# A Mamba-2 scan and a maxout FFN in one kernel: other places for scores and y, later quarter sums, a reordered load queue

## The chip, the cores and the metric

The kernel runs on one core of a Trainium2 chip. The metric is the device time of one execution in microseconds (us). Its engines are TensorE (PE in the profile, its weight loads PEld), VectorE (DVE), ScalarE (ACT), GpSimd (POOL) and SyncE (SP), which here only issues transfers. Each works through its own queue in order. Times of the kernel before: 297.39, 297.60 and 302.26 us, median 297.6.

## The reference, cut to what matters

Two blocks follow one another. The first is a chunked state-space scan over (batch 4, heads 8, sequence 768, head width 32), with a state of 16:

```python
for c in range(nc):                                   # chunks of the sequence
    cum = np.cumsum(log_a[chunk])
    L = np.exp(cum_i - cum_j) * causal                # decays
    M = (C @ B.T) * L                                 # scores, weighted
    y[chunk] = M @ x + (C @ state) * np.exp(cum)
    state = np.exp(sum(log_a)) * state + sum_j(B_j x_j * decay_from_j)
```

Its output, reshaped to 3072 tokens of 256 values, goes through a maxout FFN with d_ff = 768:

```python
h = np.maximum(np.maximum(x @ w1, x @ w2), x @ w3)
out = h @ w_out
```

The reference uses chunks of 32. The kernel takes chunks of 128 tokens, so there are NC = 6 of them.

## The kernel before

While chunk c goes through the FFN, the scan of chunk n = c + 1 is worked in between. For c = 1 to 5 a chunk takes NW = 9 *steps* k, each for two of the six blocks of d_ff and one of the three weight matrices. Chunk 0 goes before this loop; the point where the loop begins is called the seam below. The products of a step are Strassen-like: seven products in place of eight. Four of them come early and three late, and VectorE forms sums between:

```python
def early(c, k):
    A, B = (sum_bank(kind, [P, 2, HB]) for kind in "AB")      # PSUM banks: one of A, two of B
    products(c, k, [(1, A, 0), (6, A, 1), (5, B, 0), (7, B, 1)], True)        # L628
    ...
    nc.scalar.copy(out=eu[:, 0], in_=A[:, 0])                                 # L653
    nc.vector.tensor_tensor(out=eu[:, 1], in0=A[:, 1], in1=eu[:, 0], op=ALU.add)  # L654
    nc.vector.tensor_tensor(out=v, in0=B[:, 1], in1=eu[:, 1], op=ALU.add)     # L655
    nc.vector.tensor_tensor(out=t[:, 2], in0=B[:, 0], in1=v, op=ALU.add)      # L656

def late(c, k):
    products(c, k, [(2, A, 0), (3, B, 0), (4, B, 1)], False)                  # L628
    if i == 0:
        nc.scalar.copy(out=m[:, 0], in_=A[:, 0])                              # L667
    else:
        nc.vector.tensor_tensor(out=to[:, 0], in0=m[:, 0], in1=A[:, 0], op=ALU.max)   # L669
    nc.vector.tensor_tensor(out=t[:, 0:2], in0=B, in1=eu..., op=ALU.add)      # L670
    if i > 0:
        return [lambda: nc.vector.tensor_tensor(                              # L673
            out=to[:, 1:4], in0=m[:, 1:4], in1=t, op=ALU.max)]
    return []
```

What VectorE owes to the scan (score weightings, L491; sums of yT, L553; the state's sum, L462) and the maximum L673 go into a list `later`, from which each step takes a given number at three places (`pop`):

```python
def scan_weight(c, b0, r, s):                                   # L491, four to a group of scores
    M = Ls[c][:, b0:b0 + 2, 2 * r:2 * r + 2]
    nc.vector.tensor_tensor(out=M, in0=s, in1=M, op=ALU.mult)

def scores(n, b):
    for r, s in scan_scores(n, b).items():                      # TensorE, L483
        later.append(lambda r=r, s=s: scan_weight(n, b, r, s))
```

The down product (h @ w_out) is also one of seven products, in two halves u = 0, 1. Products 1, 6, 5 and 7 come first, then VectorE's *quarter sums*, then products 2, 3 and 4 into the same PSUM bank, then the rest of the sums and the store. The pieces of chunk c - 1 are handed out over the steps of chunk c, at the places marked "D":

```python
def quarter_sums(o, t):
    nc.vector.tensor_tensor(out=t[:, 0], in0=o[:, 1], in1=t[:, 1], op=ALU.add)   # L745
    nc.vector.tensor_tensor(out=t[:, 2], in0=o[:, 3], in1=t[:, 0], op=ALU.add)   # L746
    nc.vector.tensor_tensor(out=t[:, 3], in0=o[:, 2], in1=t[:, 2], op=ALU.add)   # L747

def output_products(c, u, which, kind=ffn_bank):
    if set(which) & {1, 2, 3, 4}:
        flush()                                                 # works off `behind`
    ...
    token_products(c, u, o, which)                              # L738
    if 7 in which:
        nc.scalar.copy(out=t[:, 1], in_=o[:, 0])                # L773
        behind.append(lambda: quarter_sums(o, t))
    if 4 in which:
        behind.append(lambda: output_rest(c, u, o, ob, t))      # L757, L759 and the store L786

downs.extend((c, u, which) for u, which in (
    (0, (1,)), (0, (6,)), (0, (5, 7)), (0, (2, 3, 4)), (1, (1, 6)), (1, (5, 7)), (1, (2, 3, 4))))
```

The loop, with its tables of places:

```python
X2 = ["t", "s0", "D", "D", "s2", "D", "y", "D", "D"]            # c = 2 to 4
...
for c in range(1, NC):
    for k in range(NW):
        early(c, k)
        part(n, ds[k][0]); part(n + 1, ds[k][1])                # decays: ScalarE's exps, L391
        pop(ps_[k][0])
        ...                                                     # xs[k]: D, t, s0, s2, A or y
        pop(ps_[k][1])
        maximum = late(c, k)
        ...
        if n < NC and k == 0:
            loads(c + 2)
        ...
        pop(ps_[k][2])
        flush()
        later[:0] = maximum
        if ys[k] == "D":
            down_next()
            flush()
        if k in ks and n + ks[k][0] < NC:
            decay_masks(n + ks[k][0], ks[k][1])                 # GpSimd, L384
    ...
last_output()
```

In X2, "t" is the transposes of B and C, "s0" and "s2" are the two groups of scores, and "y" is the scan's output with the state's product. Chunk 1 has its own tables X1 and P1.

Loads go through SyncE's queue in the order of the program. A tile of x has two buffers, so chunk 3's x can be loaded only when chunk 1's has been read for the last time, just ahead of the seam. The tiles of the decays and of B and C have two buffers as well:

```python
def load(c, name):
    src, w = sources[name]
    t = blocks[c][name] = raw.tile([P, BH, w], FP32, tag="raw_" + name, ...)   # bufs=2
    nc.sync.dma_start(out=t, in_=src[:, :, c * P:(c + 1) * P, :]...)           # L125

# chunk 0's FFN, n == 3:
    load(2, "B"); fetch(); load(2, "C"); fetch()
    decay_load(2, (0,)); last_load(2); decay_load(2, (2,)); load(2, "x")       # L372, L380

def loads(c):                                                   # from step 0 of the loop
    decay_load(c); last_load(c); load(c, "B"); load(c, "C"); load(c, "x")
```

And the end of the program, for the second half (u = 1) of the last chunk:

```python
    token_products(c, 1, o, (2, 3))
    nc.vector.tensor_tensor(out=t[:, 1], in0=o[:, 2], in1=t[:, 0], op=ALU.add)   # L855
    token_products(c, 1, o, (4,))
    nc.vector.tensor_tensor(out=t[:, 2], in0=o[:, 3], in1=t[:, 0], op=ALU.add)   # L857
    nc.sync.dma_start(out=rows[:, 3], in_=ob[:, 1])                              # L858
    nc.scalar.copy(out=t[:, 0], in_=o[:, 0])                                     # L859
    nc.scalar.dma_start(out=rows[:, 2], in_=ob[:, 0])                            # L860
```

Of the kernel before, what the change touches and what calls it, by code (L numbers as in the profile page):

```python
# [9 lines left out]
FP32 = mybir.dt.float32  # L10
# [3 lines left out]
ALU = mybir.AluOpType  # L14
# [5 lines left out]
def kernel(  # L20
# [20 lines left out]
    nc = tc.nc  # L41

    NB, NH, S, D = x.shape
    N = B.shape[-1]
    P = 128
    NC = S // P
# [3 lines left out]
    BH = NB * NH  # L50
# [8 lines left out]
    NQ = NF // 2  # L59
    HB = BLK // 2  # L60
# [5 lines left out]
    raw = ctx.enter_context(tc.tile_pool(name="raw", bufs=2))  # L66
    att = ctx.enter_context(tc.tile_pool(name="att", bufs=2))
    ffn = ctx.enter_context(tc.tile_pool(name="ffn", bufs=2))
# [16 lines left out]
    def att_bank(shape, name):  # L85
        turn["att"] += 1
        if shared["att"] and turn["att"] % 5 == 0:
            return bank("sumA", 1, shape, name)
        return bank("att", 4, shape, name)
# [10 lines left out]
    for k in range(REP):  # L100
# [5 lines left out]
        out=a_sb,  # L106
        in_=a_rows.rearrange("r (c i) -> (r c) i", i=P).rearrange("(w r) i -> r w i", w=2))
# [4 lines left out]
            name=nc.get_next_instruction_name(),  # L112
# [6 lines left out]
    blocks = {c: {} for c in range(NC)}  # L119
    sources = {"B": (B, N), "C": (C, N), "x": (x, D)}  # L120

    def load(c, name):
        src, w = sources[name]
        t = blocks[c][name] = raw.tile([P, BH, w], FP32, tag="raw_" + name, name="raw_" + name)
        nc.sync.dma_start(  # L125
            out=t, in_=src[:, :, c * P:(c + 1) * P, :].rearrange("b h s n -> s (b h) n"))

# [241 lines left out]
    def decay_load(c, pairs=(0, 2)):  # L369
        L = decays(c) if 0 in pairs else Ls[c]  # L370
        for b in pairs:
            nc.sync.dma_start(  # L372
                out=L[:, b:b + 2].rearrange("j b h i -> j (b h) i"),
                in_=cums[b * NH:(b + 2) * NH, c, :].partition_broadcast(P))
# [56 lines left out]
    def scan_cd(c):  # L431

        st = blocks[c]
        E = st["E"]
        st["Cd"] = Cd = att.tile([HN, NB, P], FP32, tag="Cd", bufs=1, name="Cd")
        nc.vector.tensor_tensor(out=Cd, in0=st["trC"], in1=E, op=ALU.mult)
# [197 lines left out]
    def pop(n):  # L634
        while n and later:
            later.pop(0)()
            n -= 1
# [91 lines left out]
    behind = []  # L729

    def flush():
        while behind:
            behind.pop(0)()

    def token_products(c, u, o, which, fs=range(NQ)):
        for p in which:
            for f in fs:
                nc.tensor.matmul(  # L738
                    out=o[:, PLACES[p]], lhsT=token_sums[c][p][:, f, u], rhs=wo_of(p)[:, f],
                    start=(p == 1 and f == 0), stop=True, skip_group_check=True)  # L740

    def quarter_sums(o, t):


        nc.vector.tensor_tensor(out=t[:, 0], in0=o[:, 1], in1=t[:, 1], op=ALU.add)  # L745
        nc.vector.tensor_tensor(out=t[:, 2], in0=o[:, 3], in1=t[:, 0], op=ALU.add)  # L746
        nc.vector.tensor_tensor(out=t[:, 3], in0=o[:, 2], in1=t[:, 2], op=ALU.add)  # L747

    def new_quarters(tag="ob"):
        if tag == "m":  # L750
            ob = ffn.tile([P, 4, HB], FP32, tag="m", name="m")[:, 0:2]
        else:
            ob = ffn.tile([P, 2, DM], FP32, tag="ob", bufs=2, name="ob")
        return ob, ob.rearrange("p b (m n) -> p (b m) n", n=P)
# [9 lines left out]
# [3 lines that stand above are left out]
        if 1 in which:  # L767
            halves[c, u] = kind([P, 4, P], "o")
        o = halves[c, u]
        token_products(c, u, o, which)  # L770
        if 7 in which:
            halves["ob", u] = ob, t = new_quarters()
            nc.scalar.copy(out=t[:, 1], in_=o[:, 0])  # L773
            behind.append(lambda: quarter_sums(o, t))
        if 4 in which:
            ob, t = halves["ob", u]
            behind.append(lambda: output_rest(c, u, o, ob, t))
# [57 lines left out]
    def last_output():  # L835
        c = NC - 1
        rows = out.rearrange("(b s) m -> s b m", s=S)[c * P:(c + 1) * P]
        hidden_sums(c, nc.vector, (NQ - 1, NQ))
        for u in range(2):
            third(c, u, NQ - 2)  # L840
        for p in (1, 5, 7, 6):
            for u in range(2):
                token_products(c, u, halves[c, u], (p,), (NQ - 1,))
        os = [halves[c, u] for u in range(2)]
        output_products(c - 1, 1, (4,))
        obs = [new_quarters(tag) for tag in ("ob", "m")]
        for o, (ob, t) in zip(os, obs):
            nc.scalar.copy(out=t[:, 1], in_=o[:, 0])
            quarter_sums(o, t)
        flush()  # L850
        token_products(c, 0, os[0], (2, 3, 4))
        output_rest(c, 0, os[0], *obs[0])
        o, (ob, t) = os[1], obs[1]
        token_products(c, 1, o, (2, 3))
        nc.vector.tensor_tensor(out=t[:, 1], in0=o[:, 2], in1=t[:, 0], op=ALU.add)  # L855
        token_products(c, 1, o, (4,))
        nc.vector.tensor_tensor(out=t[:, 2], in0=o[:, 3], in1=t[:, 0], op=ALU.add)  # L857
        nc.sync.dma_start(out=rows[:, 3], in_=ob[:, 1])  # L858
        nc.scalar.copy(out=t[:, 0], in_=o[:, 0])  # L859
        nc.scalar.dma_start(out=rows[:, 2], in_=ob[:, 0])  # L860


    for b in range(2, NB):
# [75 lines left out]

    def loads(c):  # L940
        if c < NC:
            decay_load(c)
            last_load(c)
            load(c, "B")
            load(c, "C")
            load(c, "x")

    def transposed(n, both=True):
        scan_b(n, att_bank)
# [9 lines left out]
    for n in range(NF * 3):  # L959
        j, g = divmod(n, 2)  # L960
        q, i = divmod(j, 3)
        f = 2 * q + g
        if n == 0:
            pair = [ffn_bank([P, BLK], "up") for _ in range(2)]
            group(pair[0], 0, 0, (0,))
            first_own((2, 3))
            group(pair[1], 0, 1, (0,))
            for p, ff in zip(pair, range(2)):
                group(p, 0, ff, (1,))
        if j > 0:  # L970
            p = ffn_bank([P, BLK], "up")
            whole_group(p, i, f)
        else:
            p = pair[g]
        if i == 0 and g == 0:
            m = ffn.tile([P, 4, HB], FP32, tag="m", name="m")
        if n in (13, 14, 16, 17):
            pop(2)
        mg = m[:, 2 * g:2 * g + 2].rearrange("p r t -> p (r t)")
        if i == 0:  # L980
            nc.scalar.copy(out=mg, in_=p)
        else:
            nc.vector.tensor_tensor(
                out=mg if i == 1 else h_of(0)[:, f], in0=mg, in1=p, op=ALU.max)
        if g == 0 and n <= 16:
            sign()
            if n <= 14:
                decode()
        if n == 1:
            fj = from_last(R, a_sb, "fj")  # L990
        if n == 3:
            first_tokens()
            load(2, "B")
            fetch()
            load(2, "C")
            fetch()
            decay_load(2, (0,))
            last_load(2)
            decay_load(2, (2,))
            load(2, "x")  # L1000
            decay_masks(1, (0, 1))
        if n == 9:
            decay_masks(1, (2, 3))
        if n in (5, 7, 9, 11, 13, 14, 15, 16):
            part(1)
        if n == 11:
            transposed(1)
            scan_c(1)
        if n == 12:
            scan_e(1)  # L1010
            scan_cd(1)
            scores(1, 0)
        if n == 15:
            shared["att"] = False
            scores(1, 2)
            places()
            weight_sums(0)
        if n == 17:
            decode()
            weight_sums(1)  # L1020
# [13 lines left out]

    X1 = ["tc", "D", "DD", "s0", "DD", "s2", "A", "y", "DD"]
    Y1 = ["", "", "D", "", "", "D", "", "D", ""]
    P1 = [(1, 0, 0), (1, 0, 0), (1, 0, 1), (1, 1, 2), (1, 0, 0), (1, 1, 3), (1, 1, 0), (1, 0, 0),
          (9, 0, 0)]
    D1 = [(0, 0), (0, 0), (2, 0), (2, 0), (2, 0), (2, 0), (0, 2), (0, 1), (0, 2)]
    K1 = {0: (0, (0, 1)), 2: (0, (2, 3)), 4: (1, (0, 1)), 6: (1, (2, 3))}  # L1040
    X2 = ["t", "s0", "D", "D", "s2", "D", "y", "D", "D"]
    Y2 = ["D", "D", "", "", "", "", "", "", ""]
    P2 = [(1, 0, 1), (1, 1, 1), (1, 0, 2), (1, 0, 0), (1, 1, 1), (1, 0, 2), (1, 0, 2), (1, 0, 2),
          (1, 0, 0)]
    D2 = [(0, 0), (1, 0), (1, 0), (1, 0)] + 5 * [(0, 1)]
    K2 = {3: (1, (0, 1)), 5: (1, (2, 3))}
# [2 lines left out]
    for c in range(1, NC):  # L1049
# [4 lines left out]
        for k in range(NW):  # L1054
# [48 lines left out]
            if n < NC and k == 2 * int(c == 1):  # L1103
                scan_e(n)
                later.append(lambda: scan_cd(n))
            pop(ps_[k][2])
            flush()
            later[:0] = maximum
            if ys[k] == "D":
                down_next()  # L1110
# [37 lines left out]
```

## Time and profile before

| | |
|---|---|
| time, median of 3 | 297.6 us |
| span of the profiled execution | 300.6 us |
| TensorE busy | 282.3 us (94%) |
| VectorE busy | 212.9 us (71%) |
| ScalarE, GpSimd busy | 119.5 us, 112.8 us |
| first step of chunk 1, 2, 3, 4, 5 in the loop | 65.1, 110.4, 157.1, 203.6, 248.8 us |
| last product ends, last store issued | 297.1, 297.8 us |

The profile is of one execution and counts from its first instruction. L628 is line 628 of the kernel before; tiles go by the program's names without buffer numbers, so `o<-wo,h` is a product of w_out and h written to a tile o. In a wait, the instruction named on the left stood at the head of its engine's queue, and the one on the right released it. The ends of matmuls are modelled in the profile, so distances are best taken from start to start.

### The profile page before, as it was taken

How to read it: one execution, taken by the hardware profiler on the slowest of the kernel's cores; microseconds unless marked ns; L12 is line 12 of the kernel's file. 1: busy time of each engine (PE TensorE's matmuls, PEld its weight loads, DVE VectorE, ACT ScalarE, POOL GpSimd, SP SyncE). 2: the span in 40 equal slices, each digit the busy share in tenths (PEclk: the TensorE clock that was granted, in tenths of full speed). 3: DMA queues.
4: the chain of work that ended last, by engine and by line, in shares of the span. 5: the costliest groups of instructions: out<-in, count | busy, mean ns of one | idle time of the engine just before them, and what ended most of it. 6: DMA issues, size and time to landing. Idle time of an engine off the chain costs nothing.

```text
span 300.6 us, 5773 instructions
## 1 busy us (share of the span) xinstructions
PE 282.3 (94%) x2204; PEld 225.9 (75%) x2204; DVE 212.9 (71%) x427; ACT 119.5 (40%) x323; POOL 112.8 (38%) x132
## 2 busy tenths in 40 slices
PE   6789999989999999899999999999989999999994
PEld 4556445478887878688977878888878888988984
DVE  2763878957789467868577868676778676677681
ACT  2946487743756345424426242525220201011101
POOL 5252656477990917900005920003530303030300
PEclk9969999999999999999999999999999999999999
DMA  7979879969787039950007690001001001000103
GB/s 90 227 248 320 181 132 178 255 173 206 210 96 106 2 96 250 106 77 2 2 0 219 145 139 27 3 0 37 0 0 37 2 1 35 2 1 0 37 0 105
DMA packets 105035, 28.15 MB, mean 94 GB/s; under 512 B 75312, under 2 KB 101936, under 8 KB 105008
## 3 DMA queue, kind: packets, MB, share of 16 engines
q1 hardware_dynamic: 104560, 27.53, 45.7%
q8 instruction: 17, 0.28, 0.4%
q10 hardware_dynamic: 448, 0.26, 0.3%
q14 instruction: 10, 0.08, 0.1%
HBM read 24.54 MB, written 3.24 MB: 92 GB/s over the span
## 4 chain that ended last, share of the span: by engine, by line
PE 77%; DVE 12%; issue 3%; DMA 3%; SPq 2%; ACT 1%; POOL 0%; DVEq 0%; ACTq 0%; POOLq 0%
PE sumB L628 22%; PE sumA L628 17%; PE o L738 15%; PE up L578 8%; PE s L483 4%; PE y L519 3%; DMA raw_x<-in_x_dram 3%; PE o L814 3%; DVE L L491 2%; PE y L506 2%; PE up L570 2%; DVE m L673 2%; PE y L530 1%; DVE rb L670 1%; SPq L125 1%
## 5 line engine op out<-in xcount | busy, mean ns | idle before, releaser
L628 PE MATMUL sumA<-yT,w 128*128 128x256 f32 x180 | 55.5, 390 | 1.4 <-DVE h L669 1.4
L653 ACT COPY eu<-sumA 128x256 f32<-128x256 f32 x45 | 16.8, 373 | 87.6 <-PE sumA L628 80.0
L391 ACT ACTIVATE L<-L,ncums 128x128 f32<-128x128 f32 x160 | 50.2, 392 | 2.5 <-POOL L L384 2.5
L628 PE MATMUL sumB<-rb 128*128 128x256 f32 x180 | 46.2, 379 | 0.0
L628 PEld LDWEIGHTS sumB<-rb 128*128 128x128 f32 x180 | 34.2, 190 | 4.7
L628 PEld LDWEIGHTS sumA<-yT,w 128*128 128x128 f32 x180 | 29.8, 190 | 9.0 <-DVE h L669 2.6
L654 DVE TENSOR_TENSOR eu<-sumA,eu 128x256 f32<-128x256 f32 x45 | 18.9, 420 | 18.9 <-ACT eu L653 18.5
L491 DVE TENSOR_TENSOR L<-s,L 128x512 f32<-128x512 f32 x46 | 29.8, 680 | 1.1 <-PE s L483 0.7
L578 PE MATMUL up<-yT,w 128*128 128x512 f32 x64 | 29.1, 600 | 0.2 <-DVE w L188 0.2
L670 DVE TENSOR_TENSOR rb<-sumB,eu 128x512 f32<-128x512 f32 x30 | 20.7, 690 | 10.4 <-PE sumB L628 10.3
L628 PE MATMUL sumB<-yT,rb 128*128 128x256 f32 x90 | 27.5, 387 | 0.6 <-DVE m L656 0.6
L185 POOL TENSOR_TENSOR w_u<-w_u,w_r 128x512 uint32<-128x512 uint32 x12 | 15.3, 1274 | 31.9 <-DVE w_u L179 15.5
L628 PE MATMUL sumB<-rb,w 128*128 128x256 f32 x90 | 26.8, 379 | 0.0
L628 PE MATMUL sumA<-rb 128*128 128x256 f32 x90 | 26.8, 379 | 0.0
L384 POOL TENSOR_SCALAR_AFFINE_SELECT L<-L 128x1024 f32<-128x1024 f32 x20 | 24.1, 1235 | 0.0
L470 POOL TENSOR_TENSOR S<-S,old 128x256 f32<-128x256 f32 x4 | 2.9, 726 | 56.2 <-DVE S L462 56.1
L713 POOL TENSOR_TENSOR L<-h 128x256 f32<-128x256 f32 x5 | 3.6, 726 | 52.2 <-DVE h L673 40.1
L655 DVE TENSOR_TENSOR v<-sumB,eu 128x256 f32<-128x256 f32 x45 | 19.1, 425 | 5.0 <-DVE eu L654 0.5
L578 PEld LDWEIGHTS up<-yT,w 128*128 128x128 f32 x64 | 11.6, 190 | 14.7 <-issue 11.7
L738 PE MATMUL o<-wo,h 128*128 128x128 f32 x120 | 17.5, 279 | 4.9 <-DVE ob L747 4.9
L738 PEld LDWEIGHTS o<-wo,h 128*128 128x128 f32 x120 | 15.9, 191 | 7.9 <-issue 5.0
L670 DVE TENSOR_TENSOR m<-sumB,eu 128x512 f32<-128x512 f32 x15 | 10.3, 690 | 15.4 <-PE sumB L628 15.3
(141 smaller groups left out, 512.5 us busy)
## 6 DMA issues: line engine op xcount, KB each, us to landing
L<-cums SPq DMA_DIRECT2D x10, 1024.0 KB, 8.8
rb<-in_moe_w_dram SPq DMA_DIRECT2D x9, 512.0 KB, 7.6
raw_x<-in_x_dram SPq DMA_DIRECT2D x6, 512.0 KB, 7.8
out_dram<-ob SPq DMA_DIRECT2D x11, 256.0 KB, 2.2
raw_B<-in_B_dram SPq DMA_DIRECT2D x6, 256.0 KB, 4.5
raw_C<-in_C_dram SPq DMA_DIRECT2D x6, 256.0 KB, 6.5
rb<-in_moe_w_out_dram SPq DMA_DIRECT2D x3, 512.0 KB, 6.0
E<-cums SPq DMA_DIRECT2D x40, 32.0 KB, 4.4
```

The costliest lines, as they stand in the source:

```text
L185: nc.gpsimd.tensor_tensor(out=u, in0=u, in1=r, op=ALU.add)
L384: nc.gpsimd.affine_select(out=Ls[c][:, b], in_=Ls[c][:, b], pattern=[[0, NH], [1, P]], compare_op=ALU.is_ge, fill=MASKED, base=0, channel_ ...
L391: nc.scalar.activation(L[:, b, h], L[:, b, h], AF.Exp, bias=ncum[c][:, b * NH + h:b * NH + h + 1], scale=1.0)
L483: nc.tensor.matmul(out=s[:, i].rearrange("j g i -> j (g i)"), lhsT=st["BT"][rows, b], rhs=st["CT"][rows, b].rearrange("p g i -> p (g i)"), ...
L491: nc.vector.tensor_tensor(out=M, in0=s, in1=M, op=ALU.mult)
L578: nc.tensor.matmul(out=bank, lhsT=w_sb[i][:, k, f * P:(f + 1) * P], rhs=yT[0][:, k], start=(k == 0), stop=(k == KD - 1))
L628: nc.tensor.matmul(out=bank[:, half], lhsT=left(p, k), rhs=sides[c][p], start=(first and half == 0), stop=True, skip_group_check=True)
L653: nc.scalar.copy(out=eu[:, 0], in_=A[:, 0])
L654: nc.vector.tensor_tensor(out=eu[:, 1], in0=A[:, 1], in1=eu[:, 0], op=ALU.add)
L655: nc.vector.tensor_tensor(out=v, in0=B[:, 1], in1=eu[:, 1], op=ALU.add)
L670: nc.vector.tensor_tensor(out=t[:, 0:2], in0=B, in1=eu[:, 1:2].to_broadcast([P, 2, HB]), op=ALU.add)
L738: nc.tensor.matmul(out=o[:, PLACES[p]], lhsT=token_sums[c][p][:, f, u], rhs=wo_of(p)[:, f], start=(p == 1 and f == 0), stop=True, skip_gro ...
```

## The change

It has four parts. In chunks 2 to 4 the second group of scores moves from step 4 to step 3, and y from step 6 to step 5. Products 2, 3, 4 of the first half of the down product then fall to step 4 and products 1, 6 of the second half to step 6. The flush that runs the quarter sums now comes ahead of a step's last pop, and is left out in step 2 of these chunks, so that the sums of the first half run at the end of step 3. The pops are arranged anew, in chunk 1 too. At the very end, product 4 of the last half goes to a PSUM bank of its own, the first quarter sum to a place of its own, and one copy and one store move ahead of it. Of the loads, chunk 2's x and the second half of its decays move from chunk 0's FFN to step 0 of the loop, behind chunk 3's x.

```diff
+    def home(c, name):
+        w = sources[name][1]
+        blocks[c][name] = raw.tile([P, BH, w], FP32, tag="raw_" + name, name="raw_" + name)
...
-    def token_products(c, u, o, which, fs=range(NQ)):
+    def token_products(c, u, o, which, fs=range(NQ), first=1):
...
-                    start=(p == 1 and f == 0), stop=True, skip_group_check=True)
+                    start=(p == first and f == 0), stop=True, skip_group_check=True)
...
-        nc.vector.tensor_tensor(out=t[:, 0], in0=o[:, 1], in1=t[:, 1], op=ALU.add)
-        nc.vector.tensor_tensor(out=t[:, 2], in0=o[:, 3], in1=t[:, 0], op=ALU.add)
+        nc.vector.tensor_tensor(out=w, in0=o[:, 1], in1=t[:, 1], op=ALU.add)
+        nc.vector.tensor_tensor(out=t[:, 2], in0=o[:, 3], in1=w, op=ALU.add)
... in last_output, w is t[:, 4] for u = 1; elsewhere t[:, 0]
-        nc.vector.tensor_tensor(out=t[:, 1], in0=o[:, 2], in1=t[:, 0], op=ALU.add)
-        token_products(c, 1, o, (4,))
-        nc.vector.tensor_tensor(out=t[:, 2], in0=o[:, 3], in1=t[:, 0], op=ALU.add)
+        nc.scalar.copy(out=t[:, 0], in_=o[:, 0])
+        nc.vector.tensor_tensor(out=t[:, 1], in0=o[:, 2], in1=t[:, 4], op=ALU.add)
+        nc.scalar.dma_start(out=rows[:, 2], in_=ob[:, 0])
+        o = att_bank([P, 4, P], "o")
+        token_products(c, 1, o, (4,), first=4)
+        nc.vector.tensor_tensor(out=t[:, 2], in0=o[:, 3], in1=t[:, 2], op=ALU.add)
         nc.sync.dma_start(out=rows[:, 3], in_=ob[:, 1])
-        nc.scalar.copy(out=t[:, 0], in_=o[:, 0])
-        nc.scalar.dma_start(out=rows[:, 2], in_=ob[:, 0])
...
     def loads(c):
         if c < NC:
+            if c == 3:
+                load(c, "x")
+                decay_load(2, (2,))
+                load(2, "x")
             decay_load(c)
             last_load(c)
             load(c, "B")
             load(c, "C")
-            load(c, "x")
+            if c > 3:
+                load(c, "x")
... chunk 0's FFN, n == 3
-            decay_load(2, (2,))
-            load(2, "x")
+            home(2, "x")
...
-    P1 = [(1, 0, 0), (1, 0, 0), (1, 0, 1), (1, 1, 2), (1, 0, 0), (1, 1, 3), (1, 1, 0), (1, 0, 0),
-          (9, 0, 0)]
+    P1 = [(1, 0, 0), (1, 0, 0), (1, 0, 1), (1, 1, 2), (1, 0, 0), (1, 1, 2), (1, 1, 1), (1, 0, 2),
+          (1, 0, 2)]
...
-    X2 = ["t", "s0", "D", "D", "s2", "D", "y", "D", "D"]
+    X2 = ["t", "s0", "D", "s2", "D", "y", "D", "D", "D"]
...
-    P2 = [(1, 0, 1), (1, 1, 1), (1, 0, 2), (1, 0, 0), (1, 1, 1), (1, 0, 2), (1, 0, 2), (1, 0, 2),
-          (1, 0, 0)]
+    P2 = [(1, 0, 1), (1, 1, 3), (0, 0, 1), (1, 1, 2), (1, 0, 0), (1, 0, 0), (9, 0, 0), (1, 0, 0),
+          (1, 0, 0)]
...
+            if not (1 < c < NC - 1 and k == 2):
+                flush()
             pop(ps_[k][2])
-            flush()
```

More of the change, by code (lines that the diff above doesn't have):

```diff
@@ L120 @@
     sources = {"B": (B, N), "C": (C, N), "x": (x, D)}
+    def home(c, name):
+        w = sources[name][1]
+        blocks[c][name] = raw.tile([P, BH, w], FP32, tag="raw_" + name, name="raw_" + name)
     def load(c, name):
-        src, w = sources[name]
-        t = blocks[c][name] = raw.tile([P, BH, w], FP32, tag="raw_" + name, name="raw_" + name)
+        if name not in blocks[c]:
+            home(c, name)
+        src, t = sources[name][0], blocks[c][name]
         nc.sync.dma_start(
@@ L739, in token_products, with quarter_sums @@
                     out=o[:, PLACES[p]], lhsT=token_sums[c][p][:, f, u], rhs=wo_of(p)[:, f],
-                    start=(p == 1 and f == 0), stop=True, skip_group_check=True)
-    def quarter_sums(o, t):
-        nc.vector.tensor_tensor(out=t[:, 0], in0=o[:, 1], in1=t[:, 1], op=ALU.add)
-        nc.vector.tensor_tensor(out=t[:, 2], in0=o[:, 3], in1=t[:, 0], op=ALU.add)
+                    start=(p == first and f == 0), stop=True, skip_group_check=True)
+    def quarter_sums(o, t, w):
+        nc.vector.tensor_tensor(out=w, in0=o[:, 1], in1=t[:, 1], op=ALU.add)
+        nc.vector.tensor_tensor(out=t[:, 2], in0=o[:, 3], in1=w, op=ALU.add)
         nc.vector.tensor_tensor(out=t[:, 3], in0=o[:, 2], in1=t[:, 2], op=ALU.add)
@@ L750, in new_quarters @@
         if tag == "m":
-            ob = ffn.tile([P, 4, HB], FP32, tag="m", name="m")[:, 0:2]
+            ob = ffn.tile([P, 4, HB], FP32, tag="m", name="m")
         else:
@@ L773, in output_products @@
             nc.scalar.copy(out=t[:, 1], in_=o[:, 0])
-            behind.append(lambda: quarter_sums(o, t))
+            behind.append(lambda: quarter_sums(o, t, t[:, 0]))
         if 4 in which:
@@ L846, in last_output @@
         obs = [new_quarters(tag) for tag in ("ob", "m")]
-        for o, (ob, t) in zip(os, obs):
+        for o, (ob, t), place in zip(os, obs, (0, 4)):
             nc.scalar.copy(out=t[:, 1], in_=o[:, 0])
-            quarter_sums(o, t)
+            quarter_sums(o, t, t[:, place])
         flush()
```

## The prediction

> **What bounds the kernel now.** I read the page first. TensorE is busy 94% of the span and no other engine over 71%, so a change can win time only where TensorE stands still.
>
> ```profile
> span 300.6 us, 5773 instructions
> PE 282.3 (94%) x2204; PEld 225.9 (75%) x2204; DVE 212.9 (71%) x427; ACT 119.5 (40%) x323; POOL 112.8 (38%) x132
> ...
> PE   6789999989999999899999999999989999999994
> ...
> PEclk9969999999999999999999999999999999999999
> ```
>
> The PE row, one digit for each 7.5 us, shows idle time in the first slices, in the ninth (60 to 67.5 us), thinly through the chunk loop, and in the last slice. The clock row dips to 6 in the third slice; the profiled execution took 302.3 us against a median of 297.6, and the change touches nothing there, so I count down from 297.6.
>
> Second, the waits of TensorE (engine, line and tile that waited, what released it: us in total, times, longest):
>
> ```profile
> PE o L738 <- DVE ob L747: 4.9, 7, 1.2
> ...
> PE o L814 <- issue: 1.5, 1, 1.5
> PE sumA L628 <- DVE h L669: 1.4, 3, 0.7
> ...
> PE sumB L628 <- DVE m L656: 0.6, 3, 0.3
> PE o L738 <- DVE m L855: 0.4, 1, 0.4
> ```
>
> The largest is the output product behind the quarter sums (L745 to L747). Third, the timeline around one such wait, TensorE first, then VectorE (start, length, operation; the bracket is the idle time ahead of it):
>
> ```profile
> 125.92 1.03 PE L628 MATMUL sumB<-rb 128*128 128x256 f32 x4
> 127.69 0.91 PE L738 MATMUL o<-wo,h 128*128 128x128 f32 x6 [0.74 <-DVE ob L747]
> ```
>
> ```profile
> 122.96 1.61 DVE L673 TENSOR_TENSOR m<-m,rb 128x768 f32<-128x768 f32 x1
> 124.50 0.41 DVE L669 TENSOR_TENSOR h<-m,sumA 128x256 f32<-128x256 f32 x1
> 124.83 0.68 DVE L670 TENSOR_TENSOR rb<-sumB,eu 128x512 f32<-128x512 f32 x1
> 125.43 1.27 DVE L491 TENSOR_TENSOR L<-s,L 128x512 f32<-128x512 f32 x2
> 126.62 0.27 DVE L745 TENSOR_TENSOR ob<-o,ob 128x128 f32<-128x128 f32 x1
> 126.93 0.29 DVE L746 TENSOR_TENSOR ob<-o,ob 128x128 f32<-128x128 f32 x1
> 127.25 0.29 DVE L747 TENSOR_TENSOR ob<-o,ob 128x128 f32<-128x128 f32 x1
> ```
>
> VectorE has no idle time here: a maximum, two score weightings and then the quarter sums stand in one queue, and products 2, 3, 4 come one step after products 5, 7, so TensorE arrives first.
>
> **What the Trainium skill says.** "TensorE: Matmul & The Clock Gate", section "Step-by-step: what each phase is for", says that only weight loads are pulled ahead and matmuls stay in program order. The trace agrees: at 127.69 the later sums, which need nothing of L747, wait too. "PSUM — Partial Sum Buffer", section "PSUM bank collisions raise a hardware error", has accesses of two engines guarded by bank, not by address. The program does so: at 296.20 product 4 waits 0.39 us for L855, which reads another quarter of the bank. "SBUF — State Buffer", section "Who interferes with whom", says that a VectorE operation with two SBUF inputs contends with a GpSimd one that reads SBUF. That fits the maximum L673: 1.61 us at 122.96 while GpSimd masks, 0.95 elsewhere. "DMA: Bandwidth & Descriptors", section "Latency and other measured facts", has HBM latency grow under load; I use it only for a rival.
>
> **Part 1: places in chunks 2 to 4 (c = 2, 3, 4).** A wait costs more than its bracket. Undisturbed, the four products of sumB are followed 0.87 us after their start; at 127.69 it was 1.77, so 0.90 lost. The same subtraction at the other five gives 0.82 (153.25), 0.89 (174.23), 0.82 (199.79), 1.34 (220.56) and 0.48 (245.37): 5.25. After each, six products took 0.74 us start to start, against 0.67: another 0.4. Together **5.7 us**. For u = 0 products 2, 3, 4 move from step 3 to step 4, with the scores between. For u = 1 the distance stays, but the sums are flushed ahead of what step 7 pops (two operations of about 0.33 us, once one), and that pop is now 0. Both should go.
>
> The maximum L673 of step 1 leaves the front of step 2, so L669 comes earlier and the products of step 3 no longer wait for it (124.96 and 171.50): start to start 0.92 and 0.99 instead of 0.43, with 0.1 each for the slower pair after: **1.2 us**.
>
> What it adds: VectorE must do in step 3 what lay over steps 2 to 4. I count from step 3's first product, with times of this trace. An undisturbed step has 1.75 us of early products, 1.30 of late ones, VectorE's eu at about 1.55 and its third sum finished 1.41 later; a score group takes 1.08. On VectorE: L670 of step 2 to 0.8, the moved maximum to 1.7, eu/v/t to 3.1, step 2's maximum to 3.9, one weighting (0.6) to 4.5, L670 to 5.1, quarter sums (0.92) to 6.0, two weightings to 7.2. TensorE starts step 4 at 4.2 and wants products 2, 3, 4 at 5.95: a wait of 0 to 0.1. The next eu starts at 7.2, its third sum is done at 8.6, and the late products of step 4 can want it at 8.4: 0.2. If the maximum meets GpSimd's masks (0.65 longer, chunks 2 and 3 only), about 0.6 more. So 0.3 to 0.9 in each of two chunks, 0.3 in the third: **1.5 us given back**.
>
> y comes a step earlier, with its four sums and the state's in step 6: five at 0.33, so eu of step 7 begins about 0.5 late, its third sum at 7.85 on a clock from step 6, when the late products want it at 7.87. Quarter sums then finish at 10.35, wanted at 10.47. Tight, but no wait.
>
> **Part 2: chunk 1's pops.** One weighting and the state's sum move behind the sums of step 6, and the four sums of yT are split between the ends of steps 7 and 8. L628's waits at 96.85 (0.33) and 110.42 (0.73) are behind exactly these. By starts: 0.49 + 0.08, and 0.89 + 0.1: **1.6 us**. The third yT sum must be ready 1.3 us into the next chunk and ends at about 1.25; I take 0.1 off.
>
> **Part 3: the end.** Product 4 of the last half gets a bank of its own, so it starts at 295.65 (0.67 after 294.98) instead of 296.20. Its sum ends at about 296.9, and the copy that ran after it (L859, 0.27) and its store move ahead. Before, the last store is issued at 297.80; now the last is at 296.9. They land in 1.7 and 1.8 us. **0.9 us.**
>
> **Part 4: the transfers.** Same bytes, other order. Before, half of chunk 2's decays is issued at 64.28, its x at 64.70, and chunk 3's x at 87.22. Now chunk 3's x goes first and waits for chunk 1's last readers (TensorE at 62.1). The two others move about 1.8 us later, the time from 64.70 to the next issue at 66.51. The masks of that half start at 79.44, x is used at 95.24; with about 9 us to land both have room. Expected: 0.
>
> Sum: 5.7 + 1.2 + 1.6 + 0.9 - 1.5 - 0.1 = 7.8 us. 297.6 - 7.8 = 289.8; I round to **290.0**.
>
> **Rivals.** *VectorE's backlog takes the wait's place.* From step 2 to step 4 it has about 13 us of work in 13.5 us of TensorE. For it: L673 at 1.61, the margins of 0.1 us above. Against: VectorE is busy 34.5 of 46.6 us in a chunk, and early in steps 5 and 7 it has slack. It would leave 3 to 4 us of the gain: 293.5 to 294.5. *The transfers are the real gain.* TensorE stands still for 1.48 us at 63.2 with no releaser, while the DMA share was 1.17 in the 2 us before; if that is instruction fetch (the page lists instruction queues among the DMA's) behind data, moving data behind the seam could free it: 288.5. Against: before, both moved transfers were issued only at 64.28 and later, when the gap was nearly over. *They do harm*: chunk 2's masks come late; 2 us at most, 292. *The waits are hidden anyway*, by clock or VectorE: then 296. Against it is the timeline, where every later start shifts.
>
> **Range and chances.** 2% is 291.65 us, a gain of 5.95. The sum holds unless given-back time exceeds 3.4 us in place of 1.6. I take **287.2 to 294.0** for 8 in 10, and chances of 0.68 faster, 0.31 within 2% and 0.01 slower: nothing adds work, so only a chain of new waits could lose.
>
> **What would show it.** Right: the wait of o on ob falls from 4.9 us to under 1 and is left only in the last output; L669's three waits go; a chunk of the loop falls from 46.6 us (110.42 to 157.06) to about 44.5; the last store is issued about 1.3 us after product 4's start, with no copy behind it. Wrong: a new line of TensorE on L656, L669 or the quarter sums in steps 3 to 7 of 1 us per chunk (rival 1); the gap at the seam gone (rival 2); a wait of GpSimd's masks or of TensorE for a DMA between 65 and 95 us (rival 3). What would make it wrong above all is the count of VectorE's backlog, where I add up margins of 0.1 us by hand.

## The result and the profile after

The changed kernel takes 291.07 us (median of 5) against 297.62 (median of 5): ratio 0.9772, 95% interval 0.9753 to 0.9792, so 6.2 to 7.3 us less. Some executions of every kernel here took about 5 us longer, and where one of them was profiled, as for before and after, the TensorE clock was near 0.5 for part of the time from 15 to 28 us and 1.0 from there on, so the ratios leave them out and the traces are compared behind that.

The page after, head and TensorE's row of 40 slices:

```profile
span 294.2 us, 5768 instructions
PE 283.0 (96%) x2204; PEld 226.0 (77%) x2204; DVE 214.0 (73%) x427; ACT 119.6 (41%) x323; POOL 113.4 (39%) x132
...
PE   6679999999999999999999999999999999999995
```

The slices of the loop are full, and the dent in the ninth is gone. The waits of TensorE after (us in total, times, longest; the first, for x, ends at 15.5 us, ahead of everything that was changed); lines are five or so higher, so L743 is L738 and L661 is L656:

```profile
PE A L456 <- DMA raw_x<-in_x_dram: 1.9, 1, 1.9
...
PE o L743 <- DVE ob L752: 1.0, 3, 0.6
...
PE sumB L633 <- DVE m L661: 0.3, 2, 0.2
```

The wait on the quarter sums fell from 4.9 us to 1.0, of which 0.57 lies in the last output. The three waits on L669, the one at the seam and the one in the end are gone.

Where the time came from, between the first products of step 0 of one chunk and the next, in us. (For before, the true first products of chunks 3 and 4 are at 156.63 and 203.17; the marks 157.06 and 203.60 used ahead are their second pair.)

| chunk | before | after | less |
|---|---|---|---|
| 1 | 45.3 | 44.2 | 1.1 |
| 2 | 46.2 | 44.7 | 1.5 |
| 3 | 46.5 | 45.1 | 1.4 |
| 4 | 45.6 | 44.1 | 1.5 |
| first L745 of the last output to last store issued | 6.65 | 5.70 | 0.95 |

Together 6.5 us, which is the timed difference. (From there to the last output both take 42.4 us.) The seam can't be read from this pair: chunk 1 begins at 65.10 and 65.18, but the trace before has a gap of 1.48 us ahead of it, and the trace after lost about as much earlier, 0.7 us of it in a longer wait for x (1.9 us against 1.2). The run with the transfers alone, below, settles it.

How steps 3 and 4 of chunk 2 look now, TensorE first and then VectorE:

```profile
126.26 0.70 PE L633 MATMUL sumA<-yT,w 128*128 128x256 f32 x2
126.90 0.70 PE L633 MATMUL sumB<-yT,rb 128*128 128x256 f32 x2
...
128.73 1.03 PE L633 MATMUL sumB<-rb 128*128 128x256 f32 x4
129.98 0.94 PE L743 MATMUL o<-wo,h 128*128 128x128 f32 x6 [0.22 <-DVE ob L752]
```

```profile
124.17 1.35 DVE L678 TENSOR_TENSOR m<-m,rb 128x768 f32<-128x768 f32 x1
...
126.76 1.12 DVE L678 TENSOR_TENSOR h<-m,rb 128x768 f32<-128x768 f32 x1
127.80 0.68 DVE L496 TENSOR_TENSOR L<-s,L 128x512 f32<-128x512 f32 x1
128.40 0.68 DVE L675 TENSOR_TENSOR m<-sumB,eu 128x512 f32<-128x512 f32 x1
129.00 0.27 DVE L750 TENSOR_TENSOR ob<-o,ob 128x128 f32<-128x128 f32 x1
```

VectorE runs on without a break from one maximum to the next, and the quarter sums, though a step away from the products 5, 7 that they follow, are still not in time: from 128.73 to 129.98 is 1.25, against 0.87 undisturbed.

### The profile page after: what moved, and what is told of

Same layout as the page of the kernel before. It is cut to its first block, busy times and chain, and to the rows that moved or that the text cites. A ratio compares the mean times of both kernels' runs of the same rounds, so it can differ in the third digit from the quotient of the medians.

```text
span 294.2 us, 5768 instructions
## 1 busy us (share of the span) xinstructions
PE 283.0 (96%) x2204; PEld 226.0 (77%) x2204; DVE 214.0 (73%) x427; ACT 119.6 (41%) x323; POOL 113.4 (39%) x132
## 3 DMA queue, kind: packets, MB, share of 16 engines
q1 hardware_dynamic: 104560, 27.53, 46.5%
## 4 chain that ended last, share of the span: by engine, by line
PE 84%; DVE 7%; DMA 3%; SPq 2%; issue 1%; ACT 1%; POOL 0%; DVEq 0%; ACTq 0%; POOLq 0%
PE sumB L633 25%; PE sumA L633 18%; PE o L743 16%; PE up L583 8%; PE s L488 4%; PE o L819 4%; PE y L524 3%; DMA raw_x<-in_x_dram 3%; PE y L511 2%; PE up L575 2%; PE y L535 1%; SPq L130 1%; PE A L456 1%; DVE rb L675 1%; DVE m L678 1%
## 5 line engine op out<-in xcount | busy, mean ns | idle before, releaser
L633 PEld LDWEIGHTS sumB<-yT,rb 128*128 128x128 f32 x90 | 15.8, 189 | 6.0 <-DVE m L661 2.3
L743 PEld LDWEIGHTS o<-wo,h 128*128 128x128 f32 x120 | 15.9, 191 | 4.0 <-DVE ob L752 1.6
L633 PEld LDWEIGHTS sumA<-rb 128*128 128x128 f32 x90 | 17.1, 190 | 2.3
```

What stands on the lines that cost most here:

```text
L633: nc.tensor.matmul(out=bank[:, half], lhsT=left(p, k), rhs=sides[c][p], start=(first and half == 0), stop=True, skip_group_check=True)
L743: nc.tensor.matmul(out=o[:, PLACES[p]], lhsT=token_sums[c][p][:, f, u], rhs=wo_of(p)[:, f], start=(p == first and f == 0), stop=True, skip ...
```

## The experiments

**Each part alone.** Four kernels, each the one before with one part of the change. For each, what was expected, then the edit and what was measured. The us less are one minus the ratio, times 297.5.

The end alone:

> The kernel before with part 3 alone (product 4 of the last half in its own bank, the copy and one store ahead of it). My theory: 0.9 us less, all of it behind the last quarter sums (from the first L745 sum of the last output to the last store issued: 5.7 us instead of 6.65), nothing elsewhere. If the end were hidden behind the stores' landing, 0 to 0.3 us.

```diff
+        nc.scalar.copy(out=t[:, 0], in_=o[:, 0])
+        nc.vector.tensor_tensor(out=t[:, 1], in0=o[:, 2], in1=t[:, 4], op=ALU.add)
+        nc.scalar.dma_start(out=rows[:, 2], in_=ob[:, 0])
+        o = att_bank([P, 4, P], "o")
+        token_products(c, 1, o, (4,), first=4)
```

Ratio 0.9961 (0.9948 to 0.9974): 0.8 to 1.5 us less. The expectation of 0.9 stands, and from the first quarter sum of the last output to the last store issued it is 5.71 us (285.82 to 291.53).

The transfers alone:

> The kernel before with part 4 alone (chunk 3's x first, chunk 2's x and half of its decays behind it). My theory: 0, within 0.4 us, and if the 1.48 us gap of TensorE at the seam is missing in the profile it is not this that removed it. Rival (the transfers are the gain): 1.5 us less, and the gap gone here while it stays in the runs that keep the old load order. Rival (they do harm): 0.5 us or more slower, with a wait for masks or a DMA between 65 and 95 us.

```diff
+            if c == 3:
+                load(c, "x")
+                decay_load(2, (2,))
+                load(2, "x")
```

Ratio 0.9998 (0.9989 to 1.0008): nothing, within 0.3 us. The gap at the seam, in the profile before, then its place here:

```profile
64.67 0.59 PE L814 MATMUL o<-wo,h 128*128 128x256 f32 x2 [1.48 <-issue]
```

```profile
58.47 0.66 PE L415 MATMUL trB<-ident,raw_B 128*128 128x128 f32 x4
58.96 1.03 PE L819 MATMUL o<-wo,h 128*128 128x256 f32 x4
```

Here it is missing, but it is missing as well in the run with only the end changed, which has the old load order:

```profile
58.50 0.66 PE L410 MATMUL trB<-ident,raw_B 128*128 128x128 f32 x4
58.99 1.03 PE L814 MATMUL o<-wo,h 128*128 128x256 f32 x4
```

Of all profiles of this study with the old load order, the profile before alone has the gap. So the old order does not bring it about each time, and the timed runs show no cost of it. What made TensorE stop there in that execution is open.

The places of chunks 2 to 4 alone:

> The kernel before with part 1 alone (places and pops of chunks 2 to 4, the flush ahead of the last pop and left out in step 2). The changed kernel's profile shows chunks 2 to 4 in 44.7, 45.1 and 44.1 us instead of 46.6, 46.5 and 45.2, so 4.4 us less less what of it came from chunk 1's last wait; I expect 4.0 to 4.4 us less. If VectorE's backlog from elsewhere set these waits, under 3 us.

```diff
-    X2 = ["t", "s0", "D", "D", "s2", "D", "y", "D", "D"]
+    X2 = ["t", "s0", "D", "s2", "D", "y", "D", "D", "D"]
... and P2 and the flush, as in the change
```

Ratio 0.9862 (0.9842 to 0.9882): 3.5 to 4.7 us less, the middle 4.1. Chunks 2 and 3 take 44.8 and 45.2 us, as in the changed kernel.

Chunk 1's pops alone:

> The kernel before with part 2 alone (the pops of chunk 1). My theory: 1.3 to 1.6 us less, the waits of TensorE for L656 in step 6 and for L669 in step 8 of chunk 1 gone. If chunk 1 is bound by its load and decode work instead, 0 to 0.5 us.

```diff
-    P1 = [..., (1, 1, 3), (1, 1, 0), (1, 0, 0), (9, 0, 0)]
+    P1 = [..., (1, 1, 2), (1, 1, 1), (1, 0, 2), (1, 0, 2)]
```

Ratio 0.9972 (0.9944 to 0.9999): 0.0 to 1.7 us less. One of the nine executions behind it, 300.03 us, makes the interval wide; the other eight took 295.7 to 296.6 us, on average 1.3 less than the kernel before. The trace agrees: chunk 1 takes 44.2 us (65.21 to 109.39) against 45.3, so 1.1, and chunk 2 another 0.1. The wait for L669 in step 8 is gone; of the wait for L656 in step 6 a rest stays (below).

The four come to 1.2 + 0.1 + 4.1 + 0.8 = 6.2 us (6.7 with 1.3 for the pops), against 6.8 for the whole: nothing of weight arises from their working together.

**Is it the places, or the order of VectorE's queue?** The scores between products 5, 7 and products 2, 3, 4 give the quarter sums more time, but the same edit also takes the pop out of their way.

> The kernel before, every place and pop as it was, with one edit: the flush that runs the quarter sums stands ahead of a step's last pop, in every step. If the distance between products 5, 7 and products 2, 3, 4 is what took the wait away (part 1 as I told it), only the second halves gain: about 0.6 us in each of three chunks, 1.8 us. Rival: what stood between was the pop, two weightings of 0.6 us each, longer than the wait of 0.7 to 1.2 us; then the first halves gain as well and it is 3.5 to 4.1 us less, as much as the moved places gave (4.1), with the two waits on L669 in step 3 still there.

```diff
-            pop(ps_[k][2])
             flush()
+            pop(ps_[k][2])
```

Ratio 0.9849 (0.9827 to 0.9871): 4.5 us less, with every place and pop as before. The rival holds: no wait of o on ob is left in the loop, and the waits on L669 are still there (1.5 us). TensorE and VectorE in step 3 of chunk 2:

```profile
121.55 1.03 PE L628 MATMUL sumB<-rb 128*128 128x256 f32 x4
122.42 0.83 PE L738 MATMUL o<-wo,h 128*128 128x128 f32 x6
```

```profile
120.45 0.68 DVE L670 TENSOR_TENSOR rb<-sumB,eu 128x512 f32<-128x512 f32 x1
121.06 0.27 DVE L745 TENSOR_TENSOR ob<-o,ob 128x128 f32<-128x128 f32 x1
...
121.90 1.28 DVE L491 TENSOR_TENSOR L<-s,L 128x512 f32<-128x512 f32 x2
```

The two weightings now stand behind the quarter sums, and product 2 starts 0.87 us after sumB's products: no wait. In the profile before they stood ahead, 1.19 us of work (125.43 to 126.62), as much as the longest of the waits (1.19). Small losses stay: step 8 takes about 5.27 us in each of the three chunks, where 5.03 is undisturbed. No run moves the places and leaves the flush behind the pop, so what the distance alone would bring is not shown; shown is that the flush does it without the distance.

**Load or order?** The same question put more sharply: in most steps VectorE has idle time just ahead of L670, as in step 7 of chunk 2 before:

```profile
150.90 0.69 DVE L670 TENSOR_TENSOR rb<-sumB,eu 128x512 f32<-128x512 f32 x1 [0.44 <-PE sumB L628]
```

Not so in step 2, where the first half's sums are due: there the long maximum makes L669 late, and L670 follows at once (124.50, 124.83).

> The kernel before, places and pops as they were, with one edit: the quarter sums are flushed inside the step, between L669 and L670, where VectorE sat idle 0.44 us for the late products of sumB. If VectorE's order and not its load bounds these chunks, the waits of o on ob in the loop go to under 0.1 us each, 5 to 5.7 us less, more than the moved places gave (4.1). If its load bounds them, the later L670 is paid back in the next step's sums, and it is 4 us or under.

```diff
             nc.vector.tensor_tensor(out=to[:, 0], in0=m[:, 0], in1=A[:, 0], op=ALU.max)
+        flush()
         nc.vector.tensor_tensor(
             out=t[:, 0:2], in0=B, in1=eu[:, 1:2].to_broadcast([P, 2, HB]), op=ALU.add)
```

Ratio 0.9788 (0.9767 to 0.9809): 5.7 to 6.9 us less, at or above the 5 to 5.7 expected. This one line, with every place and pop as before, gives nearly what the whole change gave. In step 2 of chunk 2 the sums did not fill idle time: they went ahead of L670 and of two weightings, none of which TensorE then waited for.

```profile
125.16 0.28 DVE L746 TENSOR_TENSOR ob<-o,ob 128x128 f32<-128x128 f32 x1
...
126.01 0.68 DVE L671 TENSOR_TENSOR rb<-sumB,eu 128x512 f32<-128x512 f32 x1
126.61 1.28 DVE L491 TENSOR_TENSOR L<-s,L 128x512 f32<-128x512 f32 x2
```

```profile
126.26 1.03 PE L628 MATMUL sumB<-rb 128*128 128x256 f32 x4
127.12 0.83 PE L739 MATMUL o<-wo,h 128*128 128x128 f32 x6
```

The work is the same and only its order changed, so order it is, not load. Part of the surplus over the expectation is in step 0 of chunks 3 and 4, which falls from 4.99 to 4.62 us: a wait of its late products for L656 went too. Then the maximum of step 1, moved as the change moves it:

> As the run that flushes inside the step, and the pops of steps 1 and 2 changed in chunks 2 to 4: all weightings at the end of step 1, the maximum of step 1 at the end of step 2. The waits on L669 in step 3 should go as well: about 1 us less than that run, 6 to 6.9 us less than before. If the backlog rival is right, the maximum (0.87, or 1.5 beside GpSimd's masks) shows up as a new wait of step 3's late products for L656, and nothing is gained over that run.

```diff
-    P2 = [(1, 0, 1), (1, 1, 1), (1, 0, 2), (1, 0, 0), ...
+    P2 = [(1, 0, 1), (1, 1, 3), (0, 0, 1), (1, 0, 0), ...
```

There is one execution to compare, 289.2 us, and so no interval; the trace tells more. Chunks 2, 3 and 4 take 43.7, 43.6 and 43.2 us, where the run before this one had 44.3, 44.3 and 43.2. That is 7.8 us less than in the profile before, more than the 6 to 6.9 expected; against the run before this one it is about 1.2, where about 1 was expected. VectorE in steps 2 and 3 of chunk 2:

```profile
118.69 0.42 DVE L669 TENSOR_TENSOR h<-m,sumA 128x256 f32<-128x256 f32 x1 [0.37 <-PE sumA L628]
119.03 0.28 DVE L746 TENSOR_TENSOR ob<-o,ob 128x128 f32<-128x128 f32 x1
...
119.88 0.68 DVE L671 TENSOR_TENSOR rb<-sumB,eu 128x512 f32<-128x512 f32 x1
120.48 1.06 DVE L674 TENSOR_TENSOR m<-m,rb 128x768 f32<-128x768 f32 x1
```

The quarter sums take what was idle and about 0.4 us more (L671 stands 1.19 us behind L669, where 0.83 is usual), and the moved maximum fits behind. The new wait that the backlog rival needs is not there.

And the new places with that flush:

> The kernel before with the changed kernel's places and pops for chunks 2 to 4, but the quarter sums flushed inside the step between L669 and L670, in step 2 too. If only the spot of the flush mattered, chunks 2 and 3 come to 43.6 to 43.8 us, as in the run with the old places and that flush (43.7 and 43.6): the new places are worth nothing by themselves. If the weightings they crowd into steps 3 and 4 cost time by themselves, 44.2 to 44.6 us, and the kernel is 1 to 2 us slower than that run.

```diff
+        flush()                          # in late(), between L669 and L670
... X2 and P2 as in the changed kernel, no flush left out
```

Ratio 0.9768 (0.9747 to 0.9789), about 290.6 us and so 1.4 above that run's one execution of 289.2. Chunks 2 and 3 take 44.0 us each: between my two bounds, 0.3 us more than with the old places, and chunk 4 0.1 more. All of it is in step 3 (4.53 us in chunk 2, where the step with these scores took 4.30 in the old places), and the weightings are not its cause. VectorE, then TensorE:

```profile
125.49 1.07 DVE L674 TENSOR_TENSOR m<-m,rb 128x768 f32<-128x768 f32 x1
...
127.46 0.42 DVE L656 TENSOR_TENSOR m<-sumB,v 128x256 f32<-128x256 f32 x1
127.80 1.11 DVE L674 TENSOR_TENSOR h<-m,rb 128x768 f32<-128x768 f32 x1
128.84 0.68 DVE L491 TENSOR_TENSOR L<-s,L 128x512 f32<-128x512 f32 x1
```

```profile
127.26 0.70 PE L628 MATMUL sumA<-yT,w 128*128 128x256 f32 x2
127.94 0.70 PE L628 MATMUL sumB<-yT,rb 128*128 128x256 f32 x2
```

The late products of sumB wait for L656, which stands behind the moved maximum; the first weighting comes only at 128.84. L656 ends 3.5 us after the step's first product here (124.37 to 127.88) as in the old places (119.35 to 122.85). But it is wanted at 3.43 here and was wanted at 4.17 there: the scores keep TensorE busy for 1.07 us between the early and the late products, the output products of the old place for 2.01. So once the flush is in its right spot the new places bring nothing and cost a little, because step 3 becomes too short for the maximum that was moved into it.

**A version that beats both.** Old places, old load order, the flush inside the step with its pops, the changed kernel's chunk 1 and its end; first without, then with one more bank at the end.

> The combined version without the second bank at the end (product 4 of the last chunk's first half stays behind the quarter sums). That bank should be worth 0.6 us, the 0.57 us wait: about 286.8 us here if the combined version takes 286.2. If the end is bound by VectorE's sums and the stores instead, no difference.

> A version meant to beat both: the flush inside the step with the pops of steps 1 and 2 as in the run before this, chunk 1's pops and the last half's own bank as in the changed kernel, and product 4 of the last chunk's first half in a bank of its own too, ahead of the quarter sums that TensorE waits 0.57 us for. Old places and old load order. By the sum of the parts 6.5 + 0.8 to 1.5 + 1.0 + 0.6, so 8.9 to 9.6 us less: about 288 to 289 us.

```diff
+        own = sum_bank("B", [P, 4, P])
+        token_products(c, 0, own, (4,), first=4)        # ahead of the quarter sums
         ...
-        token_products(c, 0, os[0], (2, 3, 4))
+        token_products(c, 0, o, (2, 3))
```

Ratios 0.9661 (0.9643 to 0.9680) and 0.9639 (0.9615 to 0.9663), about 287.4 and 286.8 us of 297.5. Both intervals lie below that of the changed kernel (0.9753 to 0.9792). The second is 10.7 us less, more than the 8.9 to 9.6 expected: the sum took 6.5 for chunks 2 to 4, which give 7.8. What the last bank adds can't be told from the overlapping ratios; the trace of the version with it shows it. Its end:

```profile
282.26 0.83 PE L739 MATMUL o<-wo_sums,h 128*128 128x128 f32 x6
...
282.93 0.83 PE L739 MATMUL sumB<-wo_sums,h 128*128 128x128 f32 x6
...
283.67 0.91 PE L739 MATMUL o<-wo,h 128*128 128x128 f32 x6
```

Product 4, now written to sumB's bank, runs where TensorE waited 0.57 us, and from the first quarter sum to the last store issued it is 5.04 us, against 5.70 without it.

## Why the prediction was right, and where it was off

The time, 291.07 us, lies in the range, 1.1 us above the 290.0 I named, and the gain came from the waits that I named. Off were three terms and one reason. The terms as measured, 5.7 + 1.2 - 2.7 + 1.1 + 0.95 us, give 6.3 of the 6.5.

- *The waits go, 5.7 and 1.2 us.* They went, nearly. The bound was rightly named: TensorE, held by the order of VectorE's queue. But for the first halves the reason given, that products 2, 3, 4 move a step away, was not needed: the flush ahead of the pop gives as much without it (4.5 us, interval 3.8 to 5.1, against 4.1), and in the changed kernel VectorE comes to these sums so late (129.00) that the distance is used up.
- *"Tight, but no wait" in step 8.* There is one in each chunk: at 150.71 product 2 starts 1.02 us after sumB's products, 0.15 late, and the next 0.07 later. With three chunks 0.7 us. I counted 10.35 us from step 6's first product to the end of the sums and had them wanted at 10.47. They ended at 10.47 (140.10 to 150.57), and the product began only at 150.71: I was 0.12 short, and left out the 0.14 between the end of the sum and the start of the product.
- *1.5 us given back in steps 3 and 4.* By the same subtraction about 0.8, 0.9 and 0.3 us in the three chunks, 2.0. The working was right in kind, as a late maximum costs it: beside GpSimd's masks (121.51 to 126.47) the moved one takes 1.35 us instead of 0.95, and the next, just behind them, 1.12.
- *Part 2, 1.6 us.* 1.1. The wait of step 8 is gone; step 6 kept a part of its own: its products of sumB follow those of sumA by 0.67 us (95.80 to 96.47), where 1.03 was and 0.54 is undisturbed, and the pair after by 0.12 later than before.
- *Part 3, 0.9 us.* 0.95 in the trace. *Part 4, 0.* 0.1, interval -0.2 to 0.3.

Of the rivals, VectorE's backlog took 2.7 us where I gave it 1.5, far from enough for the 293.5 to 294.5 us of that case. The one that saw the real gain in the transfers fell: moved alone they gain nothing, and the gap is missing with either order. No wait of masks or of a DMA appeared between 65 and 95 us.

## What to carry to other kernels

Where a fast engine waits for a slow one that is far from full, look at what stands ahead of the awaited operation in the slow engine's queue before giving it more distance: here one line that moved three short sums ahead of work that nobody waited for yet was worth nearly as much as a rearranged schedule. Where the slow engine itself waits for the fast one, as at L670 in most steps here, is a good spot for the awaited work. And a gap seen in one profile should be seen in a second before it is counted as a cost.

## What the runs showed of the hardware

A wait costs more than its idle time: after the waits of a product on the quarter sums the first six products took 0.74 to 0.77 us start to start instead of 0.67, and a product began 0.06 to 0.15 us after the end of the operation that released it (129.92 to 129.98 and 150.57 to 150.71 after the change, 127.54 to 127.69 before). Where the whole wait is 0.1 to 0.7 us that is a good part of it, and it decides whether a margin of 0.1 us is one.
